# Two projection units ahead of the second chunk's first states, the third and fourth block's first units exchanged, and one square of group 1 moved from ScalarE to VectorE

## The chip, the cores and the metric

The kernel runs on one core of a Trainium2 chip. A core has five engines with a queue of instructions each: TensorE (PE in the profile; its weight loads are listed as PEld), VectorE (DVE), ScalarE (ACT), GpSimd (POOL) and SyncE (SP). They run side by side and wait for each other through semaphores. Matmul results go to PSUM, which has eight banks, called 0 to 7 here; a bank can be written anew only when its last reader has finished. The metric is the device time of one execution in microseconds (us).

## The reference

Two operations follow each other. The first is a blockwise linear attention with decay over 4 batches, 8 heads, 768 positions and a head width of 64, in blocks of 64 positions:

```
intra = einsum(qb, kb) * Dmask ;  intra = einsum(intra, vb)
inter = einsum(qb * lam_pow, kv_state)
out[block] = intra + inter
kv_state = lam_block * kv_state + einsum(kb * rev_pow, vb)
```

The state is carried from block to block, so blocks are in order. The second is a two-layer network on the 3072 resulting rows of width 512:

```
h = x @ w_in                                  # 512 -> 2048
s = sin(alpha * h) ;  g = h + s * s / (alpha + 1e-9)
out = g @ w_out                               # 2048 -> 512
```

## The kernel before

The 768 positions are cut into six chunks t of 128 (two blocks of 64 each), and each chunk of all four batches gives one group g of 512 rows for the network. Work is written out by hand in one order (no scheduler moves anything), and the attention of chunk t = g + 1 is woven into the network of group g. Each engine executes its instructions in the written order.

**The network.** `hidden(g, f)` is one sixteenth of the first layer: four 128x512 matmuls into one bank (tile `hps`, L542), then the sine on ScalarE into `s_sb` (L547) and its square `s2`. `squarer(g, f)` says who squares: ScalarE (L552), or VectorE (L560), which `finish(g, f)` then issues ahead of its own operation. `finish` makes `gall = s2 * r + hps` on VectorE (L561) and so is the last reader of the bank. `project(g, m, part)` is one unit of the second layer: four 128x512 matmuls (L572) for 128 output rows m (one batch; the "block" of the title) and a quarter `part` of the 2048 columns. A block's four parts accumulate in one bank; for group 0 the banks are 6, 7, 1 and 3 for m = 0 to 3. Parts 1, 2 and 3 need the weights `w_out` 1, 2 and 3. Units are put into a list by `queue_units` and taken from its front by `run(n)`.

**The attention of a chunk** goes in two pairs of batches, pr = 0 and 1, and its two blocks of 64 positions are blk = 0 and 1. For t = 1, around the change, the order of each pair is: `turns_pair`/`turn` transposes keys and queries on TensorE (L338, L320; copies to SBUF by L344 on ScalarE and L324 on VectorE); `scores` (L443) fills two banks `F_ps`, which `masks` (L450, VectorE) multiplies into `STm`, one instruction for each bank; `states` (L423) multiplies the decayed keys `kdec` (GpSimd, L257) with `vn` into two banks `KV_ps`; `update` adds to the carried state on VectorE (L399, or L403 in four pieces) and casts it to bf16 on GpSimd (L392); `decay_state` (L388) is on GpSimd; `outputs_first`, `outputs` or, from t = 2, `outputs_in_one` (L457, L482, L505) make `O_ps`; `leave` (L524, VectorE) brings it to `xt`, the input of the next group.

**The place of the first edits.** At f = 14 of group 0 stand `scores(1, (0,), (4, 2))` and its masks, in banks 4 and 2. At f = 15 stand hidden(0, 15), one unit, `states(1, (0,), (4, 2))` in the same two banks, finish(0, 14), `update(1, 0, 0)` and finish(0, 15). After the loop come `update(1, 1, 0)`, two units, and `turns_pair(1, "k", 2, 4, (A, A))`, whose transposes go to bank 4 again. Bank 1 is last used before by hidden(0, 13), bank 3 by the transposed queries of batch 1 (`turn(1, "q", 1, 3, V)`, copied out by VectorE in L324).

**The place of the last edit.** In group 1 the chunk t = 2 is worked on: its states at f = 5, the queries of its second pair transposed on TensorE at f = 7 and copied by two ScalarE instructions (L344) ahead of the sine of f = 7, its scores at f = 8 in banks 4 to 7, the masks of pair 0 at f = 8 and of pair 1 at f = 9, the outputs at f = 11 in the same four banks. The banks of the hidden units of f = 4 to 14 rotate over three, so hidden(1, 11) waits for finish(1, 8).

**Transfers.** GpSimd issues the loads of q, k, v and the weights in its own order between its operations; `load_w_out(2)` and `load_w_out(3)` go out at f = 10 of group 0.

Of the kernel before, what the change touches and what calls it, by code (L numbers as in the profile page):

```python
# [15 lines left out]
def kernel(  # L16
# [74 lines left out]
    def load_w_out(i):  # L91
        nc.gpsimd.dma_start(out=w_out_sb[i][:],
                            in_=moe_w_out[i * 512:(i + 1) * 512, :].rearrange("(f p) d -> p f d", p=P))

    def load(t, nm, b0, b1):
        dst, src = NAT[nm]
        to = dst[t][:, b0:b1, :, :].rearrange("p b h e -> p (b h) e")
        by_head = src[b0:b1, :, t * T:(t + 1) * T, :].rearrange("b h p e -> p (b h) e")
        n = H * (b1 - b0)
        if t > 1 and nm != "v" and b0 == 2:  # L100
            nc.gpsimd.dma_start(out=to[:, 0:n - 1, :], in_=by_head[:, 1:n, :])
            nc.gpsimd.dma_start(out=to[:, n - 1:n, :], in_=by_head[:, 0:1, :])
        else:
            nc.gpsimd.dma_start(out=to, in_=by_head)  # L104
# [117 lines left out]
    V, G, A = nc.vector, nc.gpsimd, nc.scalar  # L222
# [20 lines left out]
    def home(t, blk):  # L243
        return SB[2 if blk else t % 2]
# [7 lines left out]
    def decay_k(t, b0, b1):  # L252
        if t not in kdec:
            kdec[t] = kdp.tile([P, B, H, D], BF16, name="kdec")
        R = later["R64" if t else "R128"]
        o = int(in_turn(t, b0 // 2))
        nc.gpsimd.tensor_tensor(out=kdec[t][:, b0:b1, :, :], in0=kn[t][:, b0:b1, :, :],  # L257
                                in1=R[:, o:o + H].unsqueeze(1).unsqueeze(3).broadcast_to([P, b1 - b0, H, D]),
                                op=ALU.mult)
# [56 lines left out]
    def turn(t, nm, b, n, eng):  # L316
        src, u = (kn, 0) if nm == "k" else (qn, 1)
        ps = bank("T_ps", n, BF16)[:].rearrange("p (n c i) -> p n c i", n=2, c=HP)[:, u]
        for hp in range(HP):
            nc.tensor.transpose(out=ps[:, hp, :], in_=src[t][:, b, 2 * hp:2 * hp + 2, :], identity=iden[:])  # L320
        if eng is nc.scalar:
            eng.copy(out=both[t][:, u, b, :, :], in_=ps)
        else:
            eng.tensor_copy(out=both[t][:, u, b, :, :], in_=ps)  # L324
# [4 lines left out]
    def turns_pair(t, nm, b, bk, engines):  # L329
        src, n = (kn, 0) if nm == "k" else (qn, 1)  # L330
        ps = bank("T_ps", bk, BF16)[:].rearrange("p (u c i) -> p u c i", u=2, c=HP)
        flat = src[t][:, b:b + 2].rearrange("p b h d -> p (b h) d")
        o = int(turned_by_one(t, b // 2) and not in_turn(t, b // 2))
        for u in range(2):
            for hp in range(HP):
                h = u * H + 2 * hp + o
                if h + 2 <= 2 * H:
                    nc.tensor.transpose(out=ps[:, u, hp, :], in_=flat[:, h:h + 2, :], identity=iden[:])  # L338
                else:
                    nc.tensor.transpose(out=ps[LO, u, hp, :], in_=flat[:, h, :], identity=iden[:])  # L340
                    nc.tensor.transpose(out=ps[HI, u, hp, :], in_=flat[:, 0, :], identity=iden[:])  # L341
        for u, eng in enumerate(engines):
            if eng is nc.scalar:
                eng.copy(out=both[t][:, n, b + u, :, :], in_=ps[:, u])  # L344
            else:
                eng.tensor_copy(out=both[t][:, n, b + u, :, :], in_=ps[:, u])
# [29 lines left out]
    def states1(t, pr, n):  # L376
        ps = bank("KV0_ps", n)[:].rearrange("p (u c d) -> p u c d", u=2, c=HP)
        for h in range(2 * H):
            half, m = where(1, pr, h)
            nc.tensor.matmul(out=ps[halves(half), m // HP, m % HP, :], lhsT=head(kdec, t, pr, h),  # L380
                             rhs=vn[t][:, 2 * pr + h // H, h % H, :], start=True, stop=True)
        new_state(1, pr, ps, "first")
# [4 lines left out]
    def decay_state(n, pr):  # L387
        nc.gpsimd.tensor_tensor(out=pair(SD, pr), in0=pair(S_of[n], pr), op=ALU.mult,  # L388
                                in1=L64[:, pr].unsqueeze(1).unsqueeze(3).broadcast_to([P, 2, HP, D]))

    def cast_state(n, pr, dst):
        nc.gpsimd.tensor_copy(out=pair(dst, pr), in_=pair(S_of[n], pr))  # L392
# [138 lines left out]
    def squarer(g, f):  # L531
        if g == 0:
            return V if f in (3, 5, 7, 9, 13) else A
        return A

    H0 = (0, 1, 2, 3, 5, 6, 7, 4, 0, 1, 3, 5, 0, 1, 5, 0)

    def hidden(g, f, between=None, ahead=None):
        hps = bank("hps", H0[f] if g == 0 else (0, 5, 4, 2)[f] if g == 1 and f < 4 else AB[0] if g == 1 and f == 15 else AB[f + 1] if g == 2 and f < 2 else HB[(f + 2) % 3] if g == 1 else HB[(16 * g + f + 1) % 3])
        w = w_in_sb[f // 4]  # L540
        for c in range(NDC):
            nc.tensor.matmul(out=hps[:], lhsT=w[:, c, (f % 4) * P:(f % 4 + 1) * P],  # L542
                             rhs=xt[g][:, c, :], start=(c == 0), stop=(c == NDC - 1))
        if ahead:
            ahead()
        s_sb = mlps.tile([P, GRP], BF16, name="s_sb")
        nc.scalar.activation(out=s_sb[:], in_=hps[:], func=ACTF.Sin, scale=alpha_sb[:, f:f + 1])  # L547
        if between:
            between()
        s2 = mlps.tile([P, GRP], BF16, name="s2")  # L550
        if squarer(g, f) is A:
            nc.scalar.activation(out=s2[:], in_=s_sb[:], func=ACTF.Square)  # L552
        elif squarer(g, f) is G:
            nc.gpsimd.tensor_tensor(out=s2[:], in0=s_sb[:], in1=s_sb[:], op=ALU.mult)
        hps_of[g, f] = (hps, s_sb, s2)
# [11 lines left out]
    def project(g, m, part):  # L567
        if part == 0:
            ops_of[g, m] = bank("ops", (6, 7, 1, 3)[m] if g == 0 else AB[0] if g > NT - 3 and m % 2 else OB)
        ops = ops_of[g, m]  # L570
        for f in range(4 * part, 4 * part + 4):
            nc.tensor.matmul(out=ops[:], lhsT=gall[g][:, f, m * P:(m + 1) * P],  # L572
                             rhs=w_out_sb[part][:, f % 4, :],
                             start=(f == 0), stop=(f == NFC - 1))

    def store(g, m):
        o_sb = outp.tile([P, DM], FP32, name="o_sb")
        if g < NT - 2 and (g or m < 3):
            nc.vector.tensor_copy(out=o_sb[:], in_=ops_of.pop((g, m))[:])  # L579
        else:  # L580
            nc.scalar.copy(out=o_sb[:], in_=ops_of.pop((g, m))[:])  # L581
        held.append((m * S + g * T, o_sb, 2 if g * B + m >= (NT - 1) * B - 1 else 1))
        if g:
            put_held()
# [94 lines left out]
    def queue_units(g, order):  # L679
        for m, part in order:  # L680
            def unit(g=g, m=m, part=part):
                project(g, m, part)
                if part == 3:
                    store(g, m)
            behind.append(unit)

    def run(n):
        for _ in range(min(n, len(behind))):
            behind.pop(0)()

    queue_units(0, [(0, 0), (1, 0), (2, 0), (3, 0), (0, 1), (1, 1), (2, 1), (3, 1), (0, 2), (1, 2),
                    (2, 2), (3, 2), (3, 3), (2, 3), (0, 3), (1, 3)])
    for f in range(NFC):
        hidden(0, f)
        if f in (1, 10):
            states1(0, f // 10, 2 if f == 10 else 4)
        if f == 10:
            decay_k(1, 0, 2)
            decay_state(1, 0)
            cast_state(1, 0, home(1, 0))  # L700
            load(1, "q", 2, 4)
            load_w_out(2)
            load_w_out(3)
            load(2, "v", 0, 2)
        if f in (11, 12):
            run(1)
        if f == 12:
            turns_pair(1, "k", 0, 4, (A, A))
        if f == 13:
            turn(1, "q", 0, 2, V)  # L710
            turn(1, "q", 1, 3, V)
        if f == 14:
            scores(1, (0,), (4, 2))
            masks(1, 0)
        if f == 15:
            run(1)
            states(1, (0,), (4, 2))
            finish(0, 14)
            update(1, 0, 0)
        if f != 14:  # L720
            finish(0, f)
# [1 line left out]
    decay_state(1, 1)  # L723
    cast_state(1, 1, home(1, 0))
    update(1, 1, 0)
    run(2)
    turns_pair(1, "k", 2, 4, (A, A))
    run(1)
    outputs_first(1, (0,), (5, 0))
# [127 lines left out]
```

## Time and profile before

| | us |
|---|---|
| median of the 3 runs (lowest to highest) | 206.41 (206.18 to 206.93) |
| the profiled execution's own time | 206.68 |
| its span, first to last instruction | 204.9 |
| TensorE busy in the span | 200.1 (98%) |
| ScalarE busy | 142.7 (70%) |
| VectorE busy | 132.0 (64%) |
| GpSimd busy | 106.5 (52%) |

The granted TensorE clock of the profiled execution is 1.000. The chain of work that ended last lies on TensorE for 96% of the span. A row of the chain or of a timeline gives the start in us from the first instruction, the duration in us, the engine, the line of the kernel, what it writes and reads, and how many instructions are merged into the row. In the chain, matmuls count from the modelled end of the one before to their own end, so the duration of a row holds what TensorE lost in front of it; "issue" is time for which the profile shows no waiter.

### The profile page before, as it was taken

The page shows a single profiled execution, that of the slowest core. Times are in us where ns is not written, and L with a number is a line of the kernel's source. Part 1 is how long each engine was busy: PE and PEld are TensorE (multiplying, and loading weights), DVE is VectorE, ACT ScalarE, POOL GpSimd, SP SyncE. Part 2 cuts the span into 40 slices and gives each one's busy share as a digit, 9 for nine tenths or more (in the row PEclk, how much of TensorE's full clock was granted, in tenths as well). Part 3 has the DMA queues.
Part 4 walks back from the last instruction along what each step waited for, and adds up shares of the span by engine and source line. Part 5 has one row for each costly group of instructions (what it writes and reads, how often), then busy time and mean ns, then how long its engine had stood idle before and what let it go on. Part 6 is the DMA issues. An engine that isn't in the chain of part 4 may idle for free.

```text
span 204.9 us, 5414 instructions
## 1 busy us (share of the span) xinstructions
PE 200.1 (98%) x2265; PEld 98.5 (48%) x2265; DVE 132.0 (64%) x219; ACT 142.7 (70%) x241; POOL 106.5 (52%) x112
## 2 busy tenths in 40 slices
PE   7999999999999999999999999999999999999994
PEld 2664444554455444454444454444454444444443
DVE  7795989473899969958556958555958544444000
ACT  7698997224988899676776676776666787887121
POOL 8999939989979984999966930002000000000000
PEclk9999999999999999999999999999999999999999
DMA  8999999999989999699999989601101101110313
GB/s 127 168 177 206 202 163 178 184 180 146 161 281 94 142 146 190 56 162 148 134 158 121 212 101 171 140 3 51 54 0 54 51 0 54 53 51 0 104 51 106
DMA packets 96683, 24.49 MB, mean 119 GB/s; under 512 B 87938, under 2 KB 94226, under 8 KB 96658
## 3 DMA queue, kind: packets, MB, share of 16 engines
q0 software_dynamic: 74528, 13.37, 86.5%
q1 hardware_dynamic: 22128, 10.76, 25.2%
q8 instruction: 18, 0.29, 0.6%
q14 instruction: 7, 0.06, 0.1%
q10 hardware_dynamic: 2, 0.00, 0.0%
HBM read 27.27 MB, written 6.29 MB: 164 GB/s over the span
## 4 chain that ended last, share of the span: by engine, by line
PE 96%; DVE 2%; ACT 0%; issue 0%; ACTq 0%
PE hps L542 41%; PE ops L572 40%; PE O_ps L457 2%; PE hps L139 2%; PE KV_ps L423 2%; PE hps L597 2%; PE F_ps L443 2%; PE T_ps L305 1%; PE O_ps L505 1%; PE T_ps L320 1%; DVE xt L370 1%; PE F_ps L352 1%; PE T_ps L338 1%; DVE STm L356 1%; PE KV_ps L380 0%
## 5 line engine op out<-in xcount | busy, mean ns | idle before, releaser
L561 DVE SCALAR_TENSOR_TENSOR gall<-s,r_sb,hps 128x512 bf16<-128x512 bf16 x96 | 71.2, 745 | 45.2 <-ACT s L552 45.0
L542 PE MATMUL hps<-xt,w_in 128*128 128x512 bf16 x384 | 95.5, 379 | 0.3 <-DVE xt L370 0.3
L572 PE MATMUL ops<-w_out,gall 128*128 128x512 bf16 x368 | 92.1, 379 | 0.0
L547 ACT ACTIVATE s_sb<-hps,alpha_sb 128x512 bf16<-128x512 f32 x96 | 65.2, 684 | 29.5 <-PE hps L542 29.5
L552 ACT ACTIVATE s<-s_sb 128x512 bf16<-128x512 bf16 x91 | 57.3, 629 | 2.8
L542 PEld LDWEIGHTS <-w_in 128*128 128x128 bf16 x384 | 36.6, 98 | 43.2 <-DMA w_in<-in_moe_w_in_dram 0.8
L572 PEld LDWEIGHTS <-gall 128*128 128x128 bf16 x368 | 34.8, 98 | 41.7 <-issue 0.9
L257 POOL TENSOR_TENSOR kdec<-kn,R 128x1024 bf16<-128x1024 bf16 x12 | 22.7, 1916 | 3.8 <-DMA kn<-in_k_dram 3.3
L392 POOL CAST sb<-S 128x512 bf16<-128x512 f32 x20 | 12.3, 620 | 21.0 <-DVE S L399 21.0
L388 POOL TENSOR_TENSOR SD<-S,L 128x512 f32<-128x512 f32 x16 | 16.8, 1049 | 9.0 <-DVE S L399 8.9
L524 DVE TENSOR_TENSOR xt<-O_ps,Etab 128x512 bf16<-128x512 f32 x20 | 12.8, 684 | 3.6 <-PE O_ps L482 3.5
L104 POOL DMA_DIRECT2D vn<-in_v_dram x13 | 14.6, 1135 | 0.0
L450 DVE TENSOR_TENSOR STm<-F_ps,C 128x512 bf16<-128x512 f32 x20 | 12.8, 684 | 0.9 <-PE F_ps L443 0.9
L579 DVE COPY o_sb<-ops 128x512 f32<-128x512 f32 x15 | 10.3, 689 | 4.2 <-PE ops L572 4.1
L581 ACT COPY o_sb<-ops 128x512 f32<-128x512 f32 x8 | 4.6, 577 | 11.2 <-PE ops L572 11.2
L399 DVE TENSOR_TENSOR S<-SD,KV_ps 128x512 f32<-128x512 f32 x16 | 10.8, 683 | 0.1
L104 POOL DMA_DIRECT2D kn<-in_k_dram x9 | 10.0, 1107 | 0.4 <-issue 0.3
L344 ACT COPY QKT<-T_ps 128x512 bf16<-128x512 bf16 x8 | 4.3, 586 | 5.7 <-PE T_ps L341 5.7
L139 PE MATMUL hps<-fill 128*128 128x256 bf16 (+1 forms) x24 | 6.5, 390 | 1.5 <-DVE fill L132 1.5
L104 POOL DMA_DIRECT2D qn<-in_q_dram x6 | 7.1, 1182 | 0.0
L356 DVE TENSOR_TENSOR STm<-F_ps,C 128x512 bf16<-128x512 f32 x8 | 5.2, 686 | 1.2 <-PE F_ps L352 0.8
L457 PEld LDWEIGHTS <-sb 64*64 64x64 bf16 x320 | 4.2, 107 | 3.1 <-issue 3.0
(95 smaller groups left out, 118.1 us busy)
## 6 DMA issues: line engine op xcount, KB each, us to landing
out_dram<-o_sb SPq DMA_DIRECT2D x19, 256.0 KB, 2.7
vn<-in_v_dram POOLq DMA_DIRECT2D x10, 256.0 KB, 7.8
w_out<-in_moe_w_out_dram POOLq DMA_DIRECT2D x4, 512.0 KB, 10.9
w_in<-in_moe_w_in_dram POOLq DMA_DIRECT2D x3, 512.0 KB, 10.2
kn<-in_k_dram POOLq DMA_DIRECT2D x6, 256.0 KB, 8.7
qn<-in_q_dram POOLq DMA_DIRECT2D x6, 256.0 KB, 8.9
out_dram<-o_sb SPq DMA_DIRECT2D x8, 128.0 KB, 1.8
kn<-in_k_dram POOLq DMA_DIRECT2D x4, 240.0 KB, 6.0
```

The costliest lines, as they stand in the source:

```text
L104: nc.gpsimd.dma_start(out=to, in_=by_head)
L257: nc.gpsimd.tensor_tensor(out=kdec[t][:, b0:b1, :, :], in0=kn[t][:, b0:b1, :, :], in1=R[:, o:o + H].unsqueeze(1).unsqueeze(3).broadcast_to ...
L388: nc.gpsimd.tensor_tensor(out=pair(SD, pr), in0=pair(S_of[n], pr), op=ALU.mult, in1=L64[:, pr].unsqueeze(1).unsqueeze(3).broadcast_to([P, ...
L392: nc.gpsimd.tensor_copy(out=pair(dst, pr), in_=pair(S_of[n], pr))
L399: nc.vector.tensor_tensor(out=S, in0=pair(SD, pr), in1=ps, op=ALU.add)
L450: nc.vector.tensor_tensor(out=st[:, hd], in0=att["F", t, pr, hd], op=ALU.mult, in1=of_mask(C64, t, pr, hd).unsqueeze(1).broadcast_to([P, 2 ...
L524: nc.vector.tensor_tensor(out=xview(t)[:, 2 * pr:2 * pr + 2, blk, :, :], in0=att["O", t, pr, blk], in1=Eb, op=ALU.mult)
L542: nc.tensor.matmul(out=hps[:], lhsT=w[:, c, (f % 4) * P:(f % 4 + 1) * P], rhs=xt[g][:, c, :], start=(c == 0), stop=(c == NDC - 1))
L547: nc.scalar.activation(out=s_sb[:], in_=hps[:], func=ACTF.Sin, scale=alpha_sb[:, f:f + 1])
L552: nc.scalar.activation(out=s2[:], in_=s_sb[:], func=ACTF.Square)
L561: nc.vector.scalar_tensor_tensor(out=gall[g][:, f, :], in0=s2[:], scalar=r_sb[:, f:f + 1], in1=hps[:], op0=ALU.mult, op1=ALU.add)
L572: nc.tensor.matmul(out=ops[:], lhsT=gall[g][:, f, m * P:(m + 1) * P], rhs=w_out_sb[part][:, f % 4, :], start=(f == 0), stop=(f == NFC - 1))
```

## The change

There are three edits, in two places. Of group 0's units, the first units of block 3 and of block 2 change places. At f = 15 two units instead of one are taken ahead of `states(1, (0,), (4, 2))`, and one instead of two behind it, so both (3, 0) and (2, 0) stand before the states and (0, 1) alone behind them. In group 1 the square of f = 7 is made by VectorE, at the head of finish(1, 7), instead of by ScalarE.

```diff
     def squarer(g, f):
         if g == 0:
             return V if f in (3, 5, 7, 9, 13) else A
-        return A
+        return V if (g, f) == (1, 7) else A
...
-    queue_units(0, [(0, 0), (1, 0), (2, 0), (3, 0), (0, 1), (1, 1), (2, 1), (3, 1), (0, 2), (1, 2),
+    queue_units(0, [(0, 0), (1, 0), (3, 0), (2, 0), (0, 1), (1, 1), (2, 1), (3, 1), (0, 2), (1, 2),
                     (2, 2), (3, 2), (3, 3), (2, 3), (0, 3), (1, 3)])
...
         if f == 15:
-            run(1)
+            run(2)
             states(1, (0,), (4, 2))
             finish(0, 14)
             update(1, 0, 0)
...
     update(1, 1, 0)
-    run(2)
+    run(1)
     turns_pair(1, "k", 2, 4, (A, A))
```

In the order of the instructions, the 32 state matmuls move back by one unit of four matmuls on TensorE; on VectorE one L560 is added between the state update L399 of f = 7 and finish(1, 7); on ScalarE one L552 is gone between the sines of f = 7 and f = 8. The orders of GpSimd and of SyncE are the same as before.

## The prediction

> **What bounds the kernel now.** I read the page's busy times and groups first, then the chain that ended last, whole and in short stretches around the two places of the change, and then the timelines of VectorE, ScalarE and GpSimd there. The page says that TensorE is the bound, and that the units of the second layer wait for nothing by name:
>
> ```profile
> PE 200.1 (98%) x2265; PEld 98.5 (48%) x2265; DVE 132.0 (64%) x219; ACT 142.7 (70%) x241; POOL 106.5 (52%) x112
> L572 PE MATMUL ops<-w_out,gall 128*128 128x512 bf16 x368 | 92.1, 379 | 0.0
> ```
>
> So only time that TensorE loses between its matmuls can be won, and the amount of matmul work does not change. Busy time hides such losses, since neighbouring matmuls overlap in it. The chain shows them, as a row that is longer than its like elsewhere:
>
> ```profile
> 34.00 0.04 issue
> 34.05 1.02 PE ops L572 x4
> 35.07 0.15 PE KV_ps L423 x2
> 35.22 0.03 issue
> 35.24 0.44 PE KV_ps L423 x30
> ...
> 37.51 0.39 PE T_ps L338 x7
> ...
> 41.04 0.30 PE KV_ps L423 x30
> ...
> 44.71 0.38 PE F_ps L443 x32
> ...
> 50.51 0.86 PE ops L572 x4
> ...
> 64.61 0.91 PE hps L542 x4
> 65.52 0.15 PE O_ps L457 x2
> ...
> 65.70 0.68 PE O_ps L457 x57
> ...
> 67.02 1.83 PE hps L542 x8
> ...
> 91.12 0.64 PE O_ps L457 x61
> ...
> 92.40 0.97 PE hps L542 x4
> ```
>
> There are four losses. Unit (2, 0) takes from 34.00 to 35.07, 1.07 us, where the unit at 50.51 takes 0.86: 0.21 lost. The 32 state matmuls take 0.15 + 0.03 + 0.44 = 0.62, where 32 score matmuls of the same size behind a unit take 0.38 (at 44.71): 0.24 lost. Hidden(1, 11) takes 0.91 against 0.86: 0.05 lost. The outputs of t = 2 take 67.02 - 65.52 = 1.50, those of t = 3 take 92.40 - 91.12 = 1.28: 0.22 lost. Together they are 0.72 us. VectorE tells what ended the first two:
>
> ```profile
> 31.61 0.76 DVE L324 COPY QKT<-T_ps 128x512 bf16<-128x512 bf16 x2 [0.27 <-PE T_ps L320]
> 32.32 0.89 DVE L560 TENSOR_TENSOR s<-s_sb 128x512 bf16<-128x512 bf16 x1
> 33.24 0.75 DVE L561 SCALAR_TENSOR_TENSOR gall<-s,r_sb,hps 128x512 bf16<-128x512 bf16 x1
> 33.91 1.28 DVE L450 TENSOR_TENSOR STm<-F_ps,C 128x512 bf16<-128x512 f32 x2
> ...
> 35.78 0.69 DVE L399 TENSOR_TENSOR S<-SD,KV_ps 128x512 f32<-128x512 f32 x1
> ```
>
> Finish(0, 13) ends at 33.24 + 0.75 = 33.99, and unit (2, 0), which wants its bank 1, goes on at 34.05. The second mask ends at 33.91 + 1.28 = 35.19, and the state matmuls into its bank go on at 35.24. The losses of group 1 come below.
>
> **The change part by part: the units and the states.** Nothing is added or removed; 32 matmuls move behind one more unit. Unit (3, 0) comes first and wants bank 3, which the copy that ends at 31.61 + 0.76 = 32.37 has freed: no wait at 34.00, and 0.21 is won. It ends near 34.86; unit (2, 0) then finds its bank free since 33.99 and ends near 35.72. By then both masks (35.19) are 0.5 us old, and the states run in 0.38: 0.24 is won. First part: -0.45.
>
> What comes later for it: the states end near 36.1 instead of 35.24 + 0.44 = 35.68. Behind them wait, on VectorE, update(1, 0, 0) (L399), which now starts near 36.16 instead of 35.78 and ends near 36.85, and behind it finish(0, 15) and the L403 pieces. Bank 4 is wanted by the transposes of the second keys, in the chain at 37.51 before and 37.51 - 0.45 = 37.06 after: about 0.2 to spare, so I cost it at nothing; without that cover, each us of a late update is one us of TensorE. GpSimd's queue also holds on to that update (its rows, then the keys' and weights' loads with their times to landing, then a weight load of unit (0, 2)):
>
> ```profile
> 32.33 0.60 POOL L392 CAST sb<-S 128x512 bf16<-128x512 f32 x1
> ...
> 36.71 0.67 POOL L392 CAST sb<-S 128x512 bf16<-128x512 f32 x1
> 37.28 1.95 POOL L257 TENSOR_TENSOR kdec<-kn,R 128x1024 bf16<-128x1024 bf16 x1
> 23.82 1.20 POOL L104 DMA_DIRECT2D kn<-in_k_dram  x1
> kn<-in_k_dram POOLq DMA_DIRECT2D x1, 256.0 KB, 12.9
> 34.09 1.51 POOL L92 DMA_DIRECT2D w_out<-in_moe_w_out_dram  x2
> w_out<-in_moe_w_out_dram POOLq DMA_DIRECT2D x1, 512.0 KB, 8.3
> 42.80 0.33 PEld L572 LDWEIGHTS <-gall 128*128 128x128 bf16 x3
> ```
>
> The cast can start near 36.9 instead of 36.71, and the decayed keys of pair 1 behind it end near 39.4 instead of 39.23; the next states want them at 41.04 - 0.45 = 40.59. That is 1.2 us of cover, and the loads queued behind move by 0.2 at most. Nothing is added to a DMA queue.
>
> What does not move forward is a landing. The second keys land at 23.82 + 12.9 = 36.72, ahead of 37.06. The weights `w_out` 2 land at 34.09 + 8.3 = 42.39, and unit (0, 2) loads its first stationary tile at 42.80; 0.45 earlier is 42.35. So the wait that the gain runs into is this one: 0.04, plus a late pickup like the 0.03 and 0.04 of the two "issue" rows, about 0.09. Its bounds are 0 (the landing a little earlier) and the whole 0.45 (0.36 later); I take +0.09, by the two rows themselves.
>
> **The square.** These are the rows of group 1's f = 7 to 10:
>
> ```profile
> 60.45 0.70 ACT L547 ACTIVATE s_sb<-hps,alpha_sb 128x512 bf16<-128x512 f32 x1
> 61.18 0.63 ACT L552 ACTIVATE s<-s_sb 128x512 bf16<-128x512 bf16 x1
> 60.46 0.69 DVE L399 TENSOR_TENSOR S<-SD,KV_ps 128x512 f32<-128x512 f32 x1
> 61.84 0.75 DVE L561 SCALAR_TENSOR_TENSOR gall<-s,r_sb,hps 128x512 bf16<-128x512 bf16 x1 [0.69 <-ACT s L552]
> 63.71 0.74 DVE L561 SCALAR_TENSOR_TENSOR gall<-s,r_sb,hps 128x512 bf16<-128x512 bf16 x1
> 64.36 1.28 DVE L450 TENSOR_TENSOR STm<-F_ps,C 128x512 bf16<-128x512 f32 x2
> L560 DVE TENSOR_TENSOR s<-s_sb x5: 418/418/887, 21.5 to 32.3; 128x512 bf16<-128x512 bf16 x5
> 60.38 0.61 POOL L392 CAST sb<-S 128x512 bf16<-128x512 f32 x1
> ```
>
> VectorE sits idle for 0.69 us until ScalarE's square ends at 61.18 + 0.63 = 61.81, and from then on it has no gap up to the end of the last mask, 64.36 + 1.28 = 65.64. Both losses hang on that string: finish(1, 8) ends at 63.71 + 0.74 = 64.45 and frees the bank of hidden(1, 11), and the output matmuls go on at 65.70 when the last mask has left its bank. After the change the sine ends at 61.15, L399 ends at 61.15, and VectorE squares in 0.42 (the median of its five squares), to 61.6. Finish(1, 7) starts 0.22 earlier, and so does the string: hidden(1, 11) finds its bank at 64.23 and loses nothing (-0.05); the outputs then start 0.05 earlier, come to the masked bank at 65.62, and the masks end at 65.42 (-0.22). Sum -0.27. ScalarE's 0.63 is off the path: the sine of f = 8 starts up to 0.5 earlier, and its square is there long before finish(1, 8) at 63.5. The times of this part are all counted from TensorE's arrival, so they shift together with the first part.
>
> The price of the square is 0.42 or, between the ends of that row, 0.89: at 32.32 the one long square began within 0.01 us of a GpSimd cast (32.33, 0.60 long, shown above). Here the cast at 60.38 ends at 60.99, 0.16 ahead of 61.15, and three load issues follow on GpSimd. I take 0.42, because four of five squares have it.
>
> The Trainium skill, "SBUF — State Buffer", section "Who interferes with whom", says that a VectorE instruction with both inputs in SBUF contends with a GpSimd instruction that reads SBUF, and that the one that starts second waits for the whole of the other. The long square at 32.32 agrees with it. By that rule the move would be bad wherever GpSimd computes beside it, since ScalarE's square meets nobody; what it would give here is the second rival below.
>
> **The sum.** -0.21 - 0.24 + 0.09 - 0.05 - 0.22 = -0.63 us. The profiled execution took 206.68, of which 204.9 is the span: 206.05 after, with a span near 204.3. The median of the runs is 0.27 below that execution, so the forecast is 205.8.
>
> **The rivals.** First, the next wait takes the first part's gain: `w_out` 2 or the second keys land some 0.4 us later than in this execution, or bank 4 comes late. TensorE then stands there and 0.45 is gone; only -0.27 is left, 206.1. For it speaks how close both landings are (42.39 for 42.35, 36.72 for 37.06); against it, that no issue of a load before them moves.
>
> Second, the square meets the cast and takes 0.89. Finish(1, 7) then starts at 62.09, 0.25 later than before, the string with it, and hidden(1, 11) waits 0.25 more: -0.36 + 0.25 = -0.11, 206.3. It decides from a square of 0.69 upward, the idle time that it fills. Against it speak the 0.16 us between cast and square.
>
> Third, slower: `w_out` 2 lands late in earnest. The place is unit (0, 2), the price one us of TensorE for each us after 42.35. To use up the 0.72 of gains it must land after 42.35 + 0.72 = 43.07, so 0.68 later than here. With the 10.1 us that the neighbouring transfer took,
>
> ```profile
> w_out<-in_moe_w_out_dram POOLq DMA_DIRECT2D x1, 512.0 KB, 10.1
> ```
>
> it lands at 44.19, TensorE waits 1.84, and the time is 206.41 - 0.72 + 1.84 = 207.5. Against it: the transfers ahead of it are the same ones, issued at the same times.
>
> Fourth, the states are held by something other than the masks, so that moving them does nothing: -0.21 - 0.27 = -0.48, 205.9, within my range. The match of 35.19 and 35.24 speaks against it.
>
> **How the numbers follow.** The forecast, with the small end of its gain 0.5 and the large end 0.72 (205.7 to 205.9), gets 0.59; the first rival 0.18, the second 0.11, the third 0.07, the fourth 0.05. The runs of before lie 0.23 below to 0.52 above their median, and a median of the changed kernel may sit 0.25 off; so the likeliest case alone is 205.5 to 206.1, and the range with the first two rivals is 205.4 to 206.5. A difference under 0.5%, 1.03 us, can hardly be told from no change by such runs. Faster than 205.38 needs more than every loss that I see (0.72), so only scatter and losses that I did not see give it: 0.10. Slower than 207.44 is most of the third rival: 0.06. Within 0.5%: 0.84.
>
> **What would show it.** Right: the chain has two units of 0.86 behind hidden(0, 15), 32 state matmuls in about 0.38 to 0.41 with no "issue" row, hidden(1, 11) in 0.86, and outputs of t = 2 in 1.28; L560 in group 1 lasts 0.42; finish(1, 7) follows with no idle time. Wrong: a row over 0.86 per unit at (0, 2), a longer stretch at the second keys' transposes, a square of 0.8 or more, or an output stretch that is still 1.5. The forecast would be wrong as a whole if a landing moved by a microsecond, or if a wait later in the kernel kept its absolute time, so that TensorE came to it 0.6 us early and stood there.

## The result and the profile after

The changed kernel takes 207.02 us (median of 14 runs, 206.74 to 208.05), the kernel before 206.41 (14 runs, 206.08 to 206.93). The ratio is 1.0031, with a 95% interval of 1.002 to 1.0043: slower by 0.3%, where 0.3% faster was forecast, and 0.5 us above the upper end of the range. The profiled execution took 207.0, its span is 205.1.

In this execution the first place went as forecast. This is the chain of the changed kernel from hidden(0, 15) on, with start, duration, and what ran:

```profile
32.92 0.97 PE hps L542 x4
33.89 1.73 PE ops L572 x8
35.61 0.38 PE KV_ps L423 x32
35.99 0.97 PE ops L572 x4
36.96 0.44 PE T_ps L338 x7
...
42.37 1.83 PE ops L572 x8
```

Two units in 1.73, the states in 0.38, no "issue" row between. The transposes of the second keys take 0.44 where they took 0.39, a sign that bank 4 came just in time (L399, which frees it, ends at 36.79, and they start at 36.85), and unit (0, 2) starts at 42.37 with the next one behind it in the same 1.83 as before: no wait for `w_out` 2. TensorE is 0.50 us ahead of the old trace there (42.87), and 0.54 when it starts the scores of chunk t = 2 (60.64 against 61.18).

Then it loses all of it. The chain leaves TensorE, for the square:

```profile
59.93 0.70 DVE S L399
60.62 0.02 issue
60.65 1.34 DVE s L560
61.98 0.02 issue
62.01 0.76 DVE gall L561
62.77 0.04 issue
62.81 1.02 PE hps L542 x4
63.83 0.86 PE ops L572 x4
64.69 0.99 PE hps L542 x4
65.69 0.15 PE O_ps L457 x2
65.83 0.03 issue
65.86 0.68 PE O_ps L457 x58
...
67.19 0.97 PE hps L542 x4
```

The square lasts 1.33 us, not 0.42. Finish(1, 7) ends at 62.77, and hidden(1, 10) waits for its bank. In the view of waits this is the one wait of TensorE in this stretch:

```profile
PE hps L542 <- DVE gall L561: 0.5, 1, 0.5
```

Hidden(1, 9) and (1, 10) together run from the end of the scores at 61.38 to 63.83, 2.45 us instead of 1.83; hidden(1, 11) takes 0.99 instead of 0.91; the outputs of t = 2 take 67.19 - 65.69 = 1.50 as before. So the second place costs 0.62 + 0.08 = 0.70 where 0.27 was to be won. Beside the square stood on GpSimd (timeline: start, duration, engine, line, operation):

```profile
59.84 0.60 POOL L392 CAST sb<-S 128x512 bf16<-128x512 f32 x1
60.40 1.23 POOL L104 DMA_DIRECT2D vn<-in_v_dram  x1
61.61 1.16 POOL L104 DMA_DIRECT2D kn<-in_k_dram  x1
```

If the square's own work is 0.42, it was let go at 60.65 + 1.33 - 0.42 = 61.56, just before that first load issue ends (60.40 + 1.23 = 61.63).

### The profile page after: what moved, and what is told of

Its sections match the earlier page's. It is cut to its first block, busy times and chain, and to the rows that moved or that the text cites. A ratio compares the mean times of both kernels' runs of the same rounds, so it can differ in the third digit from the quotient of the medians.

```text
span 205.1 us, 5414 instructions
## 1 busy us (share of the span) xinstructions
PE 199.7 (97%) x2265; PEld 97.7 (48%) x2265; DVE 133.4 (65%) x220; ACT 142.3 (69%) x240; POOL 106.6 (52%) x112
## 4 chain that ended last, share of the span: by engine, by line
PE 80%; POOL 6%; ACT 6%; DMA 3%; DVE 3%; issue 2%; ACTq 0%; POOLq 0%
PE ops L572 38%; PE hps L542 33%; ACT s_sb L547 3%; DMA w_in<-in_moe_w_in_dram 3%; PE O_ps L457 2%; ACT s L552 2%; PE hps L597 2%; POOL kn L104 1%; PE F_ps L443 1%; POOL vn L104 1%; PE KV_ps L423 1%; PE O_ps L505 1%; DVE gall L561 1%; POOL SD L388 1%; POOL qn L114 1%
## 5 line engine op out<-in xcount | busy, mean ns | idle before, releaser
L552 ACT ACTIVATE s<-s_sb 128x512 bf16<-128x512 bf16 x90 | 56.7, 630 | 2.8
L257 POOL TENSOR_TENSOR kdec<-kn,R 128x1024 bf16<-128x1024 bf16 x12 | 22.7, 1912 | 4.3 <-DMA kn<-in_k_dram 4.0
L399 DVE TENSOR_TENSOR S<-SD,KV_ps 128x512 f32<-128x512 f32 x16 | 10.8, 683 | 0.5 <-PE KV_ps L423 0.4
```

Source lines behind the costliest of these rows:

```text
L399: nc.vector.tensor_tensor(out=S, in0=pair(SD, pr), in1=ps, op=ALU.add)
```

## The experiments

Each ratio is to the kernel before as it ran beside that version; its median was 206.41 us beside the changed kernel and 206.47, 206.66 and 206.62 in the three sets of runs below, so versions of different sets are compared by their ratios.

**The units alone.**

```diff
-        return V if (g, f) == (1, 7) else A      # against the changed kernel
+        return A
```

> The first two edits alone; the square of f = 7 in group 1 stays on ScalarE. Theory S (the square is what costs, the units gain what was forecast): two units of 0.86 us, 32 state matmuls in 0.38, hidden(1, 11) and the outputs of t = 2 as in the kernel before (0.91 and 1.50), and about 206.0 us, 0.4 under the kernel before. Theory U (the units themselves bring the loss, because TensorE comes early to something that did not move): about 207.0, and a stretched row of the chain somewhere behind 42 us.

206.40 us, ratio to the kernel before 0.999 (0.9976 to 1.0003). So the units do not bring the loss (theory U falls). What they gain stays open here: the ratio says 0.2 us, and the interval holds nothing at all as well as the 0.4 us of theory S. Its chain has the forecast rows:

```profile
34.51 1.73 PE ops L572 x8
36.24 0.38 PE KV_ps L423 x32
```

**The square alone.**

```diff
-        return A                                 # against the kernel before
+        return V if (g, f) == (1, 7) else A
```

> The square of f = 7 in group 1 on VectorE, units as before. Theory S: the square lasts about 1.3 us as in the changed kernel, since it comes 0.25 us behind the start of the same load issue on GpSimd, and the time is 0.6 to 1.0 us over the kernel before, 207.0 to 207.4. Theory U or a chance alignment of the earlier TensorE with GpSimd: the square lasts 0.42, and the time is 206.1 to 206.4.

207.22 us, ratio 1.0033 (1.0023 to 1.0042), the same as with the units. The square is again held:

```profile
61.37 1.33 DVE L560 TENSOR_TENSOR s<-s_sb 128x512 bf16<-128x512 bf16 x1
```

It starts 0.24 behind the start of the same load issue on GpSimd (61.13), with everything 0.7 us later than in the changed kernel. So it is no chance of alignment with an earlier TensorE: square and issue keep their distance (0.25 in the changed kernel). The loss is the square's.

**What GpSimd did beside it.** First a probe with squares everywhere:

```diff
-        return V if (g, f) == (1, 7) else A
+        return V if (g, f) == (1, 7) or (g in (2, 3, 5) and f % 2) or (g == 4 and f % 2 == 0) else A
```

> A probe for durations, not for its time: the changed kernel with the squares of the odd f of groups 2, 3 and 5 and of the even f of group 4 on VectorE too, some 33 squares beside all that GpSimd does. Theory G (GpSimd holds a square with two SBUF inputs): squares beside GpSimd's casts and multiplies are long (0.8 us and more), those of group 5, where GpSimd is idle, 0.42. Whether load issues hold it too is open: five squares of group 0 took 0.42 beside load issues, the one of the changed kernel 1.33. Rival W (the wait for another instruction of VectorE, which the long ones have ahead of them, is what lasts): squares of group 5 are long too.

One execution, 207.68 us. First VectorE's group of squares in the last 44 us, where GpSimd is idle (count, busy time, mean ns):

```profile
L560 DVE TENSOR_TENSOR s<-s_sb 128x512 bf16<-128x512 bf16 x9 | 3.8, 426 | 2.9 <-ACT s_sb L547 2.9
```

Then all squares of the execution (ns, min/median/max):

```profile
L560 DVE TENSOR_TENSOR s<-s_sb x38: 415/426/1953, 21.0 to 189.1; 128x512 bf16<-128x512 bf16 x38
```

Ten of the 38 squares take 0.5 us or more, and each of the ten lies beside a GpSimd instruction; eight beside a multiply or cast, which end 0.13 to 0.14 us behind the point from which the square would need its 0.42. No square with GpSimd idle is long, so rival W falls. Load issues are mixed: most squares beside one take 0.42, but the one of group 1 takes 1.33 again, and one at 92.37 takes 1.95 beside two of them.

Then load issues on purpose, in group 5 with all its squares on VectorE, each issue behind a cast of another length or behind none:

```diff
+    def beside(f):                               # at the end of finish(5, f)
+        n = CAST.get(f)                          # columns of the cast
...
+        if n:
+            nc.vector.memset(Y[:, 0:1], 1.0)
+            nc.gpsimd.tensor_copy(out=Z[:, 0:n], in_=Y[:, 0:n])
+        else:
+            nc.vector.memset(x[:, 0, 0:1], 1.0)
+        if f != 14:
+            nc.gpsimd.dma_start(out=x[:], in_=v[0:2, :, 0:T, :].rearrange("b h p e -> p (b h) e"))
```

> A probe for durations. In group 5, where GpSimd is idle, all squares are on VectorE, and behind each of finish(5, 1) to finish(5, 14) GpSimd gets, released by a one-column memset of VectorE, a cast of 0 to 448 columns and directly behind it a load issue of 256 KB (f = 1 and 13: the issue without a cast; f = 14: a cast of 512 columns without an issue; the loaded tiles are read by nobody), so that the next square falls 0 to 0.5 us behind the start of an issue. Theory G1 (an issue that stands directly behind a cast holds the square, as in the changed kernel): the squares behind f = 2 to 12 that start inside an issue take 0.9 to 1.4 us, the ones behind f = 1 and 13 take 0.42. Theory G2 (any issue holds a square that starts in its early part): those behind f = 1 and 13 are long as well. Theory G3 (issues do not hold it, something else in group 1 does): all take 0.42, or wait for the cast at most.

```profile
L560 DVE TENSOR_TENSOR s<-s_sb 128x512 bf16<-128x512 bf16 x16 | 6.9, 429 | 7.9 <-ACT s_sb L547 7.9
```

All 16 squares of that stretch take 0.42 to 0.46, eleven of them started 0.03 to 0.19 us inside a load issue; a square of group 0 that started 0.25 us inside one (25.36 against 25.11), in the run with the square alone, took 0.42 as well. The square of group 1, in this same execution, took 1.26. G1 and G2 both fall as general rules: a load issue does not hold a square as such, nor does one that follows a cast.

**Another load in that place.** The values' load goes out at f = 5 instead of f = 6, so that the keys' issue stands behind the cast.

```diff
+            d[5] += [(new_chunk, 3), (load, 3, "v", 0, 2)]
...
-                d[6] += [(new_chunk, 3)] + [(load, 3, nm, b, b + 2) for nm, b in (("v", 0), ("k", 0), ("v", 2))]
+                d[6] += [(load, 3, nm, b, b + 2) for nm, b in (("k", 0), ("v", 2))]
```

> The changed kernel with the load of chunk 3's first values issued at f = 5 of group 1, where GpSimd is idle, instead of at f = 6; the keys' issue then stands directly behind the cast, beside the square. Theory G1 and G2: the square still takes 1.2 to 1.35 us. If it hangs on that one load, or on something that is not GpSimd's: 0.42.

The square takes 0.77, between the two answers, and ends in the midst of the keys' issue:

```profile
61.74 0.77 DVE L560 TENSOR_TENSOR s<-s_sb 128x512 bf16<-128x512 bf16 x1
61.60 1.21 POOL L104 DMA_DIRECT2D kn<-in_k_dram  x1
```

The time (207.41, one execution) is no answer, since the load also delays the multiplies of the states.

**GpSimd held back.** The direct test leaves the square where it is and takes GpSimd's work away from beside it, in order and not in content: a one-column copy that needs the result of finish(1, 7) stands behind the cast, and loads and state work follow it.

```diff
+        if t == 2 and blk == 1:                  # in update: multiply and cast
+            put_off.append(on_gpsimd)
...
-                d[6] += [(new_chunk, 3)] + [(load, 3, nm, b, b + 2) for nm, b in (("v", 0), ("k", 0), ("v", 2))]
...
+                d[6] += [(new_chunk, 3)]
...
+            if g == 1 and i == 7:                # behind finish(1, 7)
+                nc.gpsimd.tensor_copy(out=gate[:], in_=gall[1][:, 7, 0:1])
+                for nm, b in (("v", 0), ("k", 0), ("v", 2)):
+                    load(3, nm, b, b + 2)
+                while put_off:                   # decay_state and cast_state of block 1
+                    put_off.pop(0)()
```

> The changed kernel with GpSimd held back behind the cast that stands ahead of the square: a one-column copy that reads the result of finish(1, 7) comes first, then the three loads and the multiplies and casts of the second block's two updates, so that GpSimd does nothing while the square runs. Theory S with GpSimd as the holder: the square takes 0.42, hidden(1, 9) and (1, 10) take 1.83 together instead of 2.45, hidden(1, 11) 0.86, the outputs of t = 2 take 1.25 to 1.28; the end gains up to 0.9 on the changed kernel, less what GpSimd's 1.4 us of delay costs later (the decayed keys of t = 3 end near 77 us and are wanted near 76), so 206.0 to 206.8. If something other than GpSimd holds the square: 1.3 us again.

```profile
60.05 0.61 POOL L392 CAST sb<-S 128x512 bf16<-128x512 f32 x1
62.12 0.19 POOL L833 COPY gate<-gall 128x1 bf16<-128x1 bf16 x1 [1.47 <-DVE gall L569]
...
60.85 0.42 DVE L568 TENSOR_TENSOR s<-s_sb 128x512 bf16<-128x512 bf16 x1
61.31 0.75 DVE L569 SCALAR_TENSOR_TENSOR gall<-s,r_sb,hps 128x512 bf16<-128x512 bf16 x1
```

With GpSimd idle the same square takes 0.42, with the same L399 directly ahead of it, and hidden(1, 9) to (1, 11) run without a wait; the outputs of t = 2 take 66.50 - 65.15 = 1.35 from the end of hidden(1, 11) to their own, against 67.03 - 65.52 = 1.51 in the kernel before. GpSimd is the holder, by its own work and not by a transfer that it started: in the probe with squares everywhere no DMA packet at all moves from 61.08 to 62.0, while the square of group 1 is held. The time missed its forecast, 207.54 us (ratio 1.0054, 1.0029 to 1.0079), 0.9 above the kernel before. The delay comes back at t = 3, where the view of waits has 1.1 us; less the 0.05 and 0.16 won at hidden(1, 11) and the outputs, that is about the difference (an estimate). Its runs lie between 207.2 and 209.7, but for one of 212.0. The wait:

```profile
PE KV_ps L423 <- POOL kdec L257: 1.1, 1, 1.1
```

**The gain of the units, in two more executions.** The kernel before, unchanged.

> The kernel before, unchanged, for a second look at what it loses at unit (2, 0) and the states of the first pair. In the first look it was 0.21 + 0.24; in the run with the square alone, whose units stand as before, 0 + 0.16. If the loss is fixed: 0.45 again. If it depends on how early TensorE comes against the landing of the second chunk's keys, which sets the cast that holds the square of f = 13: anything from 0 to 0.5, the smaller the later TensorE comes to hidden(0, 15).

> The kernel before, unchanged, a third look at what it loses at unit (2, 0) and the states. If it is set by how far TensorE is ahead of the landing of the keys, the square of f = 13 ends within 0.3 us behind the end of the cast again, and the loss lies between 0 and 0.45; 0.45 in this look too would speak for a fixed loss.

The second execution (206.17 us) and the third (206.39), unit (2, 0) and the states in the chain:

```profile
33.83 0.86 PE ops L572 x4
34.69 0.48 PE KV_ps L423 x32
```

```profile
34.11 0.86 PE ops L572 x4
34.98 0.39 PE KV_ps L423 x32
```

They lose 0.10 and 0.01, where the first execution lost 0.45. What sets it is the square of f = 13 in group 0. In the third execution (VectorE, then GpSimd):

```profile
32.43 0.46 DVE L560 TENSOR_TENSOR s<-s_sb 128x512 bf16<-128x512 bf16 x1
32.01 0.60 POOL L392 CAST sb<-S 128x512 bf16<-128x512 f32 x1
```

It ends at 32.89, and the cast at 32.61. In the first execution the same square lasted 0.89 and ended at 33.21, the cast at 32.93: 0.28 behind the cast in both. Finish(0, 13) and the masks follow that square. The cast ends a string on GpSimd that starts when the second chunk's first keys land (its multiply L257 waits for them in all traces). So the loss hangs on how far TensorE is behind that cast. In the five profiled executions with the old order of units (us):

| run | L257 starts (keys landed) | cast ends | hidden(0, 15) starts | distance | lost |
|---|---|---|---|---|---|
| before, first | 29.48 | 32.93 | 33.03 | 0.10 | 0.45 |
| square alone | 29.64 | 33.09 | 33.47 | 0.38 | 0.16 |
| before, second | 28.97 | 32.42 | 32.86 | 0.44 | 0.10 |
| before, third | 29.16 | 32.61 | 33.14 | 0.53 | 0.01 |
| copy alone (below) | 28.86 | 32.31 | 32.85 | 0.54 | 0 |

Distance and loss add up to 0.54 or 0.55 in each. The small losses come in part from a later TensorE and in part from an earlier landing: in the second execution TensorE came 0.17 earlier than in the first, but the keys landed 0.51 earlier.

**A better relief for ScalarE.** The second copy of the transposed queries reads PSUM:

```diff
-            d[7] += [(put_held,), (turns_pair, 2, "q", 2, AB[0], (A, A))]     # units as changed, square on ScalarE
+            d[7] += [(put_held,), (turns_pair, 2, "q", 2, AB[0], (A, V))]
```

> The first two edits, the square on ScalarE, and of the two copies of the transposed queries ahead of the sine of f = 7 the second one on VectorE instead of ScalarE. It reads PSUM, so by the rule that two SBUF inputs contend with GpSimd it meets nobody. Theory S with that rule: the copy takes about 0.4 us, finish(1, 7) starts some 0.4 us earlier against the scores than in the kernel before, hidden(1, 11) takes 0.86, the outputs of t = 2 take 1.28, and the time is 0.2 to 0.3 us under the first run of this set: 205.7 to 205.8. Rival: every VectorE instruction in this place is held by GpSimd's load issues: the copy takes over 1 us, and the time is 206.2 or more.

206.21 us, ratio 0.9991 (0.9975 to 1.0007): 0.19 under the units alone, about as expected, but not 205.7. The copy takes 0.42 beside GpSimd's multiply and cast, and the second place loses nothing more:

```profile
60.02 0.42 DVE L346 COPY QKT<-T_ps 128x512 bf16<-128x512 bf16 x1
```

```profile
64.33 0.86 PE hps L542 x4
65.19 0.64 PE O_ps L457 x61
...
66.48 1.62 PE hps L542 x7
```

Outputs 66.48 - 65.19 = 1.29. The same copy with the units as before:

> The kernel before with the second copy of the transposed queries on VectorE and nothing else; the units stand as before. The outputs of t = 2 should fall from 1.50 to about 1.28 and hidden(1, 11) to 0.86 as in the run with units and copy, so 0.2 to 0.27 under the kernel before, 206.2. If the units are worth 0.1 to 0.2 on the median, it is that much slower than the run with both; if they are worth nothing, equal to it.

206.35 us, ratio 0.9984 (0.9968 to 1.0). Here too unit (2, 0) and the states lose nothing in the profiled execution (0.86 and 0.38). With and without the units the two runs cannot be told apart. And the copy with the units and the square of f = 13 on ScalarE:

```diff
-            return V if f in (3, 5, 7, 9, 13) else A
+            return V if f in (3, 5, 7, 9) else A
```

> The run with the copy on VectorE, and the square of f = 13 in group 0 on ScalarE instead of VectorE. That square lasts 0.49 to 0.89 in all traces so far, and it ends 0.28 behind the end of a GpSimd cast each time. If that hold is what delays finish(0, 13), the masks and so TensorE where the units stand, finish(0, 13) starts 0.2 to 0.4 earlier; but with the two units ahead of the states TensorE no longer waits there, so the time stays within 0.2 of the run with the copy alone, 206.0 to 206.3. If ScalarE's 0.63 more delays the sine of f = 14 and the copies, 206.4 or more.

206.24 us, ratio 0.9978 (0.9968 to 0.9987): the one version of the set that is faster than both kernels beyond its interval. Finish(0, 13) does not start earlier against the cast in it (0.39 us behind its end, 0.32 with the copy and the square on VectorE), so the expected mechanism is not what helped; that it is better than the copy alone is not shown.

## Why the prediction was wrong

**What bounds the kernel.** Right: all that was won or lost lay between TensorE's matmuls, and the chain named each place.

**The first two losses, 0.21 + 0.24.** They were read rightly, with the waits that ended them, but their size belongs to that execution and not to the kernel: five executions with the old unit order lost 0.45, 0.16, 0.10, 0.01 and 0 there. This term of the sum was mis-sized. In place of -0.45 the ratios give about -0.04 us (1.0031 against 1.0033, both with the square), -0.2 (0.999) and +0.14 (0.9991 against 0.9984, both with the copy), each with 0.3 to 0.5 us of uncertainty. The rows say much the same: 0.14 lost on the mean of the five, less 0.05 at bank 4, so about 0.1 us to win (an estimate). The profiled execution was 0.27 us above its own median; I used that to shift the result and did not ask whether the shift sat in the very rows that I was counting.

**What comes later for it.** Right in the main: bank 4 just in time (0.05 lost, costed at nothing), GpSimd's queue covered, and no wait for `w_out` 2, for which 0.09 was taken.

**The square at 0.42.** This is the step that failed: "I take 0.42, because four of five squares have it". It took 1.33, 1.33, 1.33 and 1.26 in the four executions with GpSimd's queue as it was. A choice by neighbours would not have found this: three of the four short squares stood beside load issues, as the new one does, and nothing in the trace of the kernel before shows that an issue can hold a square. What the long one did show is that GpSimd can. The upper end that I kept, 0.89, was too low: I took the longest row for the longest possible.

**The string behind it.** Right in its form, as the run with GpSimd held back shows: with the square at 0.42, hidden(1, 11) and the outputs won 0.05 and 0.16 of the forecast 0.05 and 0.22. But one link was left out. The bank of hidden(1, 10) is freed by finish(1, 7), and I had priced only hidden(1, 11). In the changed kernel that link came first and cost 0.62.

**The rivals.** The second had the place and the holder's engine, and a price of +0.25 from a square of 0.89; with 1.33 and the missing link the second place cost +0.70. It named the cast; the cast was over by 0.2 us, and the square was held to the end of the load issue behind it. The first, third and fourth did not come about.

**Squares beside GpSimd.** In the probe eight squares beside multiplies and casts were long, those with GpSimd idle took 0.42, and so did the copy from PSUM beside a multiply and a cast. The Trainium skill, "SBUF — State Buffer", section "Who interferes with whom", has a VectorE instruction with two inputs in SBUF contend with GpSimd's reads; these rows agree. The same section infers that such an instruction does not meet the writing of descriptors; eleven squares inside load issues in group 5 agree, the one of group 1 does not.

**The sum.** By rows, the changed kernel's trace has -0.45 + 0.05 for the first place and +0.70 for the second, +0.3, as its profiled execution shows against that of before (207.0 and 206.68). By the ratios the first place is worth nearly nothing and the second 0.7 us by the square alone (1.0033 of 206.5); the result is 0.6.

**What stays open.** Why this load issue held the square, to its end with the values' load and to about 0.5 us behind its start with the keys' load, and the issues of group 5 and of group 0 did not. The runs show that neither a cast ahead of the issue, nor its distance from the square, nor which load it is decides this alone; the multiply ahead of the cast and the state of the load queue were not tried.

## What to carry to other kernels

Set what a move can win against what it can lose. Here a square of 0.42 could win 0.27 and no more, while each us by which it outlasts the 0.69 us of idle time costs TensorE about as much (1.33 cost 0.70); one long row among five is a warning, and its length is no upper end. Before work goes to VectorE, look at what GpSimd does at that moment; an instruction that reads PSUM relieved ScalarE here at no cost, one with two SBUF inputs did not. And a wait on a timed landing that one profile shows is worth taking away only if a second profile shows it too: here it was 0.45 us in one execution and nothing in another.

## What was not expected of the hardware

A square of 0.42 us was held for 0.9 us in the changed kernel by a GpSimd instruction whose only work is to issue a 256 KB load, the same in four executions to 0.07 us (1.26 to 1.33). Squares beside GpSimd's multiplies and casts were let go 0.13 to 0.14 us ahead of the end that the profile gives for the GpSimd instruction, in all eight cases of the probe (its spans on GpSimd are rough). And the hold works both ways: a GpSimd cast that began beside a running square took 0.83 instead of 0.60 in the probe, and two more took 0.80.

```profile
89.32 0.50 DVE L560 TENSOR_TENSOR s<-s_sb 128x512 bf16<-128x512 bf16 x1
89.45 0.83 POOL L392 CAST sb<-S 128x512 bf16<-128x512 f32 x1
```
